# P of the row tile that TensorE turns over, kept as float32 in a range of its own, with float32 products for its columns

## The chip, the core and the metric

One NeuronCore of a Trainium2 chip runs the kernel alone. Times are device microseconds from start to end of an execution. The engines are named as the profile names them: PE (TensorE; PEld is its weight load), DVE (VectorE), ACT (ScalarE), POOL (GpSimd) and SP, whose queue issues all DMAs.

## What is computed

Attention over 2 batches and 8 heads of 768 positions of width 64, in which a query sees only the keys of its own hash bucket, and then two feed-forward layers over the 1536 tokens.

```python
q_bits = (einsum('bhsd,dk->bhsk', q, proj) > 0); k_bits = (einsum('bhsd,dk->bhsk', k, proj) > 0)
mask = q_bucket[:, :, :, None] == k_bucket[:, :, None, :]
scores = where(mask, scale * matmul(q, k.T), -1e9)
attn = exp(scores - max(scores)); attn = attn / (sum(attn) + 1e-09)
x = matmul(attn, v)                      # then [1536, 512]
h = x @ w_in;  g = maximum(0.01 * h, h);  x = g @ w_out
h = x @ w_in2; g = maximum(h, 0) + alpha * minimum(h, 0);  out = g @ w_out2
```

All inputs are float32, except that the weights come as 64-bit words which the kernel converts itself.

## The kernel before

The heads go in eight pairs (`NP`, index `i`), the two heads of a pair being `j` = 0 and 1. For each pair `load` fetches q, k and V, `split_qk` splits q and k in high and low parts, `turn` transposes them on PE (tp), and `bits` makes the bucket bits (bp). `split_v` scales V by a power of two and splits it into two float16 tiles (vb: high, low). `score` is called 12 times per pair, once per tile of 128 rows and head; three row tiles (`t` = 0, 1, 2) make a half `f` of the positions. One score is four matmuls into PSUM (sc, L685), a minimum on DVE that also moves the tile to SBUF as s (L692), and an exp in place on ACT (L695).

P must lie with the keys on the partitions for the product with V. Two of three row tiles are split into a high and a low float16 part on ACT, POOL or DVE (hl; L734, L740 and the helpers at L399 and L402) and transposed by a DMA (L746). The third, marked "T" in `HI_ON` (t = 2; in the last half of the last pair also t = 1, by `HI_LAST`), is turned over by PE: three transposes of 128 columns into a PSUM tile (pp, L711), of which there is one; then ACT writes the high float16 part out of PSUM (L715), and DVE the low one, which is the difference (L719). All three row tiles share the tile pt, [128, 24, 384] float16, whose last axis is the rows.

`pv` multiplies: for each of the six blocks of 128 keys, three float16 products (V high by P high, V low by P high, V high by P low), each for both heads, of 384 columns (L778). The heads write partitions 0 to 63 and 64 to 127 of one PSUM tile (o). The inverse row sums are laid along by three transposes (pr, L769), scaled on ACT together with the powers of two of V and P (rs, L772), and DVE multiplies o by rs into x (L787).

After that come the FFN units: `convert` makes float16 high and low weights (L927 to L971), `split` does the same to x (L978, L985), `h_group` and `y_group` do the matmuls (`three`, L1029 to L1031).

The order of the work on each engine is set by a planner: every step is put in with `plan.add(claim, ways, reads, writes)`; `Plan.order` lists the steps by a model of engine times, first forwards and then in passes from the back and the front, and takes the best end. A step with several ways (vec is DVE, act ACT, gps POOL) may go to any of these engines. A `Ring` of n tiles lets the step that takes tile n + 1 wait until the first is free: there are 6 tiles of s (`SB`), 3 of pt, 1 of V's float32 tile (rv). The FFN reuses the ring of s for g and ts.

Of the kernel before, what the change touches and what calls it, by code (L numbers as in the profile page):

```python
# [9 lines left out]
F32 = mybir.dt.float32  # L10
# [24 lines left out]
LO_LAST = "P-DP-DP-D---"  # L35
SB = 6


HOP, HOP_PE, LANDING = 0.12, 0.29, 1.6
PATIENCE, PASSES = 0.2, 8  # L40

# [131 lines left out]
class Plan:  # L173
# [49 lines left out]
    def order(self):  # L223

        self.link()
        for n, op in enumerate(self.ops):
            op.n = n
        end = self.first()
        best = end, [(op.start, op.way) for op in self.ops]
        for _ in range(PASSES):  # L230
            self.late(end)
            end = self.early()
            if end < best[0]:
                best = end, [(op.start, op.way) for op in self.ops]
        for op, (op.start, op.way) in zip(self.ops, best[1]):
            pass
        self.end = best[0]
        return sorted(self.ops, key=lambda op: (op.start, op.n))

    def first(self):  # L240

        lines = Lines()
        ready = [op for op in self.ops if not op.left]
        while ready:
            found = [(lines.soonest(op, True), op) for op in ready]
            first = {}
            for (at, *_, k), op in found:
                eng = op.ways[k][0]
                first[eng] = min(first.get(eng, at), at)
            eng = min(first, key=first.get)  # L250
            (at, done, x, k), op = min(
                (f for f in found if f[1].ways[f[0][3]][0] == eng and f[0][0] <= first[eng] + PATIENCE),
                key=lambda f: (f[1].turn, f[1].claim, f[1].n),
            )
# [37 lines left out]
def lsh_attention_ffn_kernel(  # L292
# [53 lines left out]
    nat_r = dict(zip("kq", ring("nat", 1, "kq")))  # L346
    rv_r = ring("rv", 1)
    rb_r, rs_r = ring("rb", 1, ("rb", "rs"))
# [59 lines left out]
    st_raw, st_nat, st_op, st_bt, st_v = {}, {}, {}, {}, {}  # L408
    sums, pts = {}, {}

# [106 lines left out]
    def turn(i):  # L517
# [3 lines left out]
        for nm, hi, sc in (("k", 64, -scale), ("q", 0, 1.0)):  # L521
            n = st_nat.pop((nm, i))
            for j in range(2):
                a, bb = ops[j][nm + "a"], ops[j][nm + "b"]
                for f in range(2):
# [18 lines left out]
                    for dst, src, wr in to:  # L544
                        ways = [act(0.49, lambda dst=dst, src=src, sc=sc: nc.scalar.activation(
                            out=dst(), in_=src(), func=AF.Copy, scale=sc))]
                        if i == 0:
                            ways.append(vec(0.61, lambda dst=dst, src=src, sc=sc:
                                nc.vector.tensor_scalar_mul(dst(), src(), sc)))
                        plan.add(at, ways, [ps], [wr])  # L550
                    at += 0.7
                if i:
                    plan.add(
                        at,
                        dma(1.2, lambda bb=bb: bb.t[0:64].bitcast(F32),
                            lambda a=a, hi=hi: a.t[hi:hi + 64].bitcast(F32)),
                        [a], [(bb, (0, 2))],
                    )
# [55 lines left out]
    def split_v(i):  # L614
        r_ = st_raw.pop(("v", i))
        vb = v_r.new([128, 2, 2, T, D], F16, "vb")
# [22 lines left out]
        def scales():  # L639
# [13 lines left out]
             act(0.94, lambda: nc.scalar.activation(  # L653
                 out=part(0), in_=r(), func=AF.Copy, scale=c.t[:, 0:1]))],
            [r_, c], [(vb, (0, 1))],
        )
        def p_lo():
            gmul(r(), r(), c.t[:, 0:1])
            gsub(part(1), r(), part(0))

        plan.add(
            at + 2,
            [vec(1.25, lambda: nc.vector.scalar_tensor_tensor(
                out=part(1), in0=r(), scalar=c.t[:, 0:1], in1=part(0), op0=ALU.mult,
                op1=ALU.subtract), True), gps(2.6, p_lo)],
            [c, (vb, (0, 1))], [r_, (vb, (1, 2))], lean=LEAN_V,
        )

    def score(g):
# [12 lines left out]
        def go():  # L682
# [14 lines left out]
            accum_out=sm.t[:, t, j:j + 1])), [mn], [s, (sm, (2 * t + j, 2 * t + j + 1))])  # L697
        hi_eng, lo_eng = (HI_ON[m], LO_ON[m]) if i < NP - 1 else (HI_LAST[m], LO_LAST[m])
        ts = slice(t * 128, t * 128 + 128)
        if hi_eng == "T":  # L700
            for h in range(2):
                ps = p_ps.new([128, TH, 128], F32, "pp")
                c0 = 2 * T * j + h * TH

                def hi(c0=c0):
                    return pt.t[:, c0:c0 + TH, ts]

                def over(ps=ps, h=h):
                    for c in range(TH):
# [21 lines left out]
        if lo_eng == "P":  # L731
# [3 lines left out]
                "P": gps(0.84, lambda: gmul(hi(), s.t, by))}  # L735
        plan.add(g + 1, [ways["A"]] if lo_eng == "P" else list(ways.values()), [s], [hw])
        if lo_eng == "P":
# [5 lines left out]
        if j == 1:  # L743
            plan.add(
                g + 2,
                ("SP", 3.7, 4.0, lambda: nc.sync.dma_start_transpose(  # L746
                    out=pt.t[:, :, ts], in_=hl.t.rearrange("p j s -> p (j s)"))),
                [hl], [(pt, (64 * t, 64 * t + 64))],
            )

    def pv(i, f):
# [14 lines left out]
        def along():  # L766
# [450 lines left out]
```

## Time and profile before

| what | us |
|---|---|
| median of 3 runs | 777.45 (775.96 to 778.15) |
| profiled execution | 779.42 |
| its span, first to last instruction | 777.6 |
| PE busy | 729.4 (94%) |
| DVE busy | 606.0 (78%) |
| ACT busy | 478.2 (61%) |
| POOL busy | 316.1 (41%) |

The span has two parts: attention up to about 265 us, where four engines and the DMAs work side by side, and the FFN after that. Shares over the whole span mix the two, so the rows below go by stretches. Matmuls are pipelined: the duration of one is longer than the distance from its start to the start of the next, so a run of them is read from start to start.

### The profile page before, as it was taken

The page shows a single profiled execution, that of the slowest core. Times are in us where ns is not written, and L with a number is a line of the kernel's source. Part 1 is how long each engine was busy: PE and PEld are TensorE (multiplying, and loading weights), DVE is VectorE, ACT ScalarE, POOL GpSimd, SP SyncE. Part 2 cuts the span into 40 slices and gives each one's busy share as a digit, 9 for nine tenths or more (in the row PEclk, how much of TensorE's full clock was granted, in tenths as well). Part 3 has the DMA queues.
Part 4 walks back from the last instruction along what each step waited for, and adds up shares of the span by engine and source line. Part 5 has one row for each costly group of instructions (what it writes and reads, how often), then busy time and mean ns, then how long its engine had stood idle before and what let it go on. Part 6 is the DMA issues. An engine that isn't in the chain of part 4 may idle for free.

```text
span 777.6 us, 12424 instructions
## 1 busy us (share of the span) xinstructions
PE 729.4 (94%) x4465; PEld 461.4 (59%) x4465; DVE 606.0 (78%) x1196; ACT 478.2 (61%) x923; POOL 316.1 (41%) x345
## 2 busy tenths in 40 slices
PE   7888988899978689999999999999999999999997
PEld 6676757777755346666666666565555555555553
DVE  5998979899998998787787876998687777853332
ACT  5988778788878556655434434556776664554341
POOL 3896667767543242434322233232322222222221
PEclk8999999999989899999999999999999999999999
DMA  6699879987957531222403303020140320000112
GB/s 183 147 198 200 169 150 197 195 166 148 197 101 186 152 109 45 92 82 78 140 1 110 109 1 103 25 90 0 55 136 28 109 81 28 28 1 1 42 40 82
DMA packets 131213, 77.87 MB, mean 100 GB/s; under 512 B 100864, under 2 KB 123392, under 8 KB 131152
## 3 DMA queue, kind: packets, MB, share of 16 engines
q1 hardware_dynamic: 131152, 77.08, 39.5%
q8 instruction: 35, 0.57, 0.3%
q14 instruction: 26, 0.21, 0.1%
HBM read 43.00 MB, written 3.15 MB: 59 GB/s over the span
## 4 chain that ended last, share of the span: by engine, by line
PE 77%; DVE 13%; ACT 4%; DMA 2%; issue 2%; POOL 1%; SPq 0%; ACTq 0%; DVEq 0%
PE y L1029 11%; PE y L1031 11%; PE y L1030 11%; PE h L1029 10%; PE h L1031 10%; PE h L1030 10%; PE o L778 5%; PE sc L685 4%; DVE s L692 3%; PE bp L569 2%; PE pp L711 2%; DMA pt<-hl 2%; ACT s L695 1%; PE tp L530 1%; DVE pt L719 1%
## 5 line engine op out<-in xcount | busy, mean ns | idle before, releaser
L402 POOL TENSOR_TENSOR gs<-ts,gs 128x384 f16<-128x384 f32 x128 | 122.6, 959 | 314.1 <-ACT gs L1064 249.4
L1029 PE MATMUL h<-x,wn 128*128 128x384 f16 x512 | 167.6, 327 | 5.2 <-DVE ts L1052 3.9
L1030 PE MATMUL h<-x,wn 128*128 128x384 f16 x512 | 167.5, 327 | 0.0
L1031 PE MATMUL h<-x,wn 128*128 128x384 f16 x512 | 167.4, 327 | 0.0
L1064 ACT CAST gs<-ts 128x384 f16<-128x384 f32 x128 | 65.3, 511 | 51.5 <-DVE ts L1061 27.9
L695 ACT ACTIVATE s<-s,mn 128x768 f32<-128x768 f32 x96 | 89.4, 932 | 8.7 <-DVE s L692 8.5
L692 DVE TENSOR_SCALAR_CACHE_REDUCE s<-sc 128x768 f32<-128x768 f32 x96 | 89.6, 948 | 3.8 <-PE sc L685 3.4
L1061 DVE SCALAR_TENSOR_TENSOR ts<-ts,nal 128x384 f32<-128x384 f32 x64 | 39.5, 616 | 64.8 <-ACT ts L1057 40.4
L1029 PE MATMUL y<-gs,wp 128*128 128x384 f16 x256 | 83.5, 326 | 0.0
L1030 PE MATMUL y<-gs,wp 128*128 128x384 f16 x256 | 83.5, 326 | 0.0
L1031 PE MATMUL y<-gs,wp 128*128 128x384 f16 x256 | 83.5, 326 | 0.0
L1100 DVE SCALAR_TENSOR_TENSOR x<-y,back,x 128x384 f32<-128x384 f32 (+1 forms) x84 | 56.6, 674 | 33.0 <-PE y L1031 32.5
L1050 ACT ACTIVATE ts<-h 128x384 f32<-128x384 f32 x64 | 31.0, 487 | 74.2 <-PE h L1031 59.8
L1030 PEld LDWEIGHTS <-wn 128*128 128x128 f16 x512 | 50.3, 98 | 40.6 <-issue 6.0
L1029 PE MATMUL y<-wp,gs 128*128 128x512 f16 x192 | 72.8, 379 | 0.0
L1030 PE MATMUL y<-wp,gs 128*128 128x512 f16 x192 | 72.8, 379 | 0.0
L1031 PE MATMUL y<-wp,gs 128*128 128x512 f16 x192 | 72.8, 379 | 0.0
L1029 PEld LDWEIGHTS <-wn 128*128 128x128 f16 x512 | 50.2, 98 | 35.5 <-issue 0.6
L1031 PEld LDWEIGHTS <-wn 128*128 128x128 f16 x512 | 50.3, 98 | 33.4 <-issue 0.5
L685 PE MATMUL sc<-ka,qa 128*128 128x384 f32 x192 | 58.2, 385 | 10.2 <-DVE s L692 9.8
L402 POOL TENSOR_TENSOR hl<-s,hl 128x768 f16<-128x768 f32 x31 | 54.2, 1750 | 30.9 <-ACT hl L734 30.7
L1057 ACT ACTIVATE ts<-h,al_s 128x384 f32<-128x384 f32 x64 | 37.0, 577 | 44.6 <-PE h L1031 25.0
(154 smaller groups left out, 1475.4 us busy)
## 6 DMA issues: line engine op xcount, KB each, us to landing
wr<-in_moe_w_out_dram SPq DMA_DIRECT2D x19, 512.0 KB
wr<-in_moe_w_in_dram SPq DMA_DIRECT2D x17, 512.0 KB
r<-in_moe_w_in_dram SPq DMA_DIRECT2D x15, 512.0 KB
r<-in_moe_w_out_dram SPq DMA_DIRECT2D x13, 512.0 KB
v<-in_v_dram SPq DMA_DIRECT2D x8, 384.0 KB
out_dram<-x SPq DMA_DIRECT2D x12, 256.0 KB
k<-in_k_dram SPq DMA_DIRECT2D x7, 384.0 KB
q<-in_q_dram SPq DMA_DIRECT2D x7, 384.0 KB
```

The lines of the kernel that those rows point to most:

```text
L402: nc.gpsimd.tensor_tensor(out=o, in0=a, in1=b, op=ALU.subtract)
L685: nc.tensor.matmul(sc.t[:, h, 0:HALF], lhsT=o[a].t[0:rows, row:row + 128], rhs=o[b].t[0:rows, h * HALF:h * HALF + HALF], start=(n == 0), s ...
L692: plan.add(g, vec(1.03, lambda: nc.vector.tensor_scalar(out=s.t.rearrange("p (a b) -> p a b", a=2), in0=sc.t[:, :, 0:HALF], scalar1=FILL, ...
L695: plan.add(g, act(1.12, lambda: nc.scalar.activation(out=s.t, in_=s.t, func=AF.Exp, scale=-1.0, bias=mn.t[:, 0:1], accum_out=sm.t[:, t, j: ...
L778: nc.tensor.matmul(ps.t[64 * j:64 * j + 64], lhsT=vb.t[:, piece, j, c, :], rhs=pt.t[:, 2 * T * j + o + c, :], start=(c + n == 0), stop=(c ...
L1029: nc.tensor.matmul(ps, lhsT=lh[0], rhs=rh[0], start=first, stop=False)
L1030: nc.tensor.matmul(ps, lhsT=lh[0], rhs=rh[1], start=False, stop=False)
L1031: nc.tensor.matmul(ps, lhsT=lh[1], rhs=rh[0], start=False, stop=last)
L1057: plan.add(claim, act(0.58, lambda: nc.scalar.activation(out=g.ap(F32), in_=ps.t, func=AF.Relu, scale=al_s.t[:, 0:1])), [ps, al_s], [g.use()])
L1061: plan.add(claim, vec(0.57, lambda: nc.vector.scalar_tensor_tensor(out=g.ap(F32), in0=lo.ap(F32), scalar=nal.t[:, f:f + 1], in1=g.ap(F32), ...
L1064: plan.add(claim, act(0.51, lambda: nc.scalar.copy(out=gh.ap(), in_=g.ap(F32))), [g.use()], [gh.use()])
L1100: plan.add(claim, vec(0.69 if l else 0.56, lambda: nc.vector.scalar_tensor_tensor(out=a(), in0=ps(), scalar=c(), in1=a(), op0=ALU.mult, op ...
```

## The change

A turned row tile of P is no longer split. It stays float32 in an unbroken range of pt, the bytes that its two float16 parts would fill, so `whole` sees them as [128, 12, 128] float32. The tiles that the DMA transposes are packed in front of them (`narrow`, `kept` of them, 128 columns each). After the three transposes there is one copy out of PSUM on ACT (`FP` = 0), and no step on DVE.

In `pv` the six float16 products of a block of keys go over the `kept` columns only, 256 of 384 (128 in the last half of the last pair). For each turned row tile two products follow, one per head, with V's raw float32 tile (v32) as weights and the float32 P as columns. Since neither is scaled there, the inverse row sums are scaled in two pieces, by inv for the first columns and by 1 for the rest, each on ACT or DVE (`FR` = 1).

V's float32 tile now lives until the products, so its ring has 2 tiles; the ring of s has 5 instead of 6, which also makes the slots of g 8 instead of 10. V's low part loses its way over POOL, which overwrote the raw tile. The planner now tries six values of `PATIENCE` with six passes each, where it had one value and eight passes, and it keeps the best. The options `FT`, `FH`, `FV` and `FB` are 0 and leave their lists of ways as they were.

```diff
-SB = 6
+SB = 5
+FT, FP, FR, FH, FV, FB = 0, 0, 1, 0, 0, 0
...
-PATIENCE, PASSES = 0.2, 8
+PATIENCE, PASSES = (0.05, 0.1, 0.15, 0.2, 0.25, 0.3), 7
...
-    rv_r = ring("rv", 1)
+    rv_r = ring("rv", 2)
...
+    def kept(i, f):
+
+        return sum(engines(i)[0][6 * f + m] != "T" for m in range(6)) // 2
+
+    def narrow(pt, i, f):
+
+        n = 128 * kept(i, f)
+        return pt.t.rearrange("p a b -> p (a b)")[:, 0:4 * T * n].rearrange("p (a b) -> p a b", a=4 * T)
+
+    def whole(pt, t):
+
+        flat = pt.t.rearrange("p a b -> p (a b)")[:, 4 * T * 128 * t:4 * T * 128 * (t + 1)]
+        return flat.bitcast(F32).rearrange("p (a b) -> p a b", a=2 * T)
...
-                w = (t * 64 + c0, t * 64 + c0 + TH)
-                plan.add(g + 1 + h / 2, act(0.49, lambda ps=ps, hi=hi: nc.scalar.mul(hi(), ps.t, PSCALE)),
-                         [ps], [(pt, w)])
-                plan.add(
-                    g + 1.4 + h / 2,
-                    vec(0.56, lambda ps=ps, hi=hi, c0=c0: nc.vector.scalar_tensor_tensor(
-                        out=pt.t[:, c0 + T:c0 + T + TH, ts], in0=ps.t, scalar=PSCALE, in1=hi(),
-                        op0=ALU.mult, op1=ALU.subtract)),
-                    [ps, (pt, w)], [(pt, (w[0] + T, w[1] + T))],
-                )
+                w = [(pt, (t * 64 + 2 * c0, t * 64 + 2 * (c0 + TH)))]
+                plan.add(g + 1 + h / 2, [
+                    act(0.49, lambda ps=ps, out=out: nc.scalar.copy(out=out(), in_=ps.t)),
+                    vec(0.56, lambda ps=ps, out=out: nc.vector.tensor_copy(out(), ps.t)),
+                ][:1 + FP], [ps], w)
...
-        plan.add(at, act(0.58, lambda: nc.scalar.activation(
-            out=rs.t, in_=pr.t, func=AF.Copy, scale=inv.t[:, i:i + 1])), [pr, (inv, (i, i + 1))], [rs])
+        split = 128 * kept(i, f)
+        for c0, c1 in ((0, split), (split, HALF)):
+            by = lambda c0=c0: inv.t[:, i:i + 1] if c0 == 0 else 1.0
+            dur = 0.26 + (c1 - c0) * 0.00083
+            plan.add(at, [
+                act(dur, lambda c0=c0, c1=c1, by=by: nc.scalar.activation(
+                    out=rs.t[:, c0:c1], in_=pr.t[:, c0:c1], func=AF.Copy, scale=by())),
+                vec(dur, lambda c0=c0, c1=c1, by=by: nc.vector.tensor_scalar_mul(
+                    rs.t[:, c0:c1], pr.t[:, c0:c1], by())),
+            ][:1 + FR], [pr, (inv, (i, i + 1))], [(rs, (c0, c1))])
+        v32 = st_v32[i]
...
-                            ps.t[64 * j:64 * j + 64],
+                            ps.t[64 * j:64 * j + 64, 0:split],
...
-                            rhs=pt.t[:, 2 * T * j + o + c, :],
+                            rhs=narrow(pt, i, f)[:, 2 * T * j + o + c],
...
-            plan.add(at + c / 4, pe(0.49, go), [vb, pt], [ps])
+                for t in range(split // 128, TH):
+                    for j in range(2):
+                        nc.tensor.matmul(
+                            ps.t[64 * j:64 * j + 64, t * 128:t * 128 + 128],
+                            lhsT=v32.t[:, j, c, :], rhs=whole(pt, t)[:, T * j + c],
+                            start=False, stop=(c == T - 1), skip_group_check=True,
+                        )
+
+            plan.add(at + c / 4, pe(0.55 + 0.025 * (TH - split // 128), go), [vb, pt, v32], [ps])
```

The planner's new order moves steps everywhere. On DVE, in the second pair of heads, this stands in the kernel before (s,mn<-sc is a score's minimum, pt<-pp the low half of a turned tile, hl<-s,hl that of a tile for the DMA, x<-o,rs the end of a block of products):

```order
L740 SCALAR_TENSOR_TENSOR hl<-s,hl 128x768
L663 SCALAR_TENSOR_TENSOR vb<-v,c,vb 128x768
L719 SCALAR_TENSOR_TENSOR pt<-pp,pt 128x3x128
L579 TENSOR_SCALAR bt<-bp,least,weight 128x384 x2
L692 TENSOR_SCALAR s,mn<-sc 128x768
L761 RECIPROCAL sum<-sum 128x6
L787 TENSOR_TENSOR x_1_125<-o,rs 128x384
L692 TENSOR_SCALAR s,mn<-sc 128x768
L719 SCALAR_TENSOR_TENSOR pt<-pp,pt 128x3x128
L692 TENSOR_SCALAR s,mn<-sc 128x768
```

and this about the same place in the changed one:

```order
L755 SCALAR_TENSOR_TENSOR hl<-s,hl 128x768
L776 RECIPROCAL sum<-sum 128x6
L971 SCALAR_TENSOR_TENSOR r<-r 128x512
L586 TENSOR_SCALAR bt<-bp,least,weight 128x384 x2
L712 TENSOR_SCALAR s,mn<-sc 128x768
L818 TENSOR_TENSOR x_1_125<-o,rs 128x384
L712 TENSOR_SCALAR s,mn<-sc 128x768
L794 TENSOR_SCALAR rs<-pr,inv 128x256
L712 TENSOR_SCALAR s,mn<-sc 128x768
```

The low halves pt<-pp are gone from the row, and scalings of the row sums (rs<-pr,inv) and an integer pass over a weight tile (r<-r) stand in it. Counted over the whole order, DVE has 68 pt<-pp less, 12 rs of 256 columns and 10 of 128 more, and 5 vb<-v,c, 2 x splits and a few casts more.

On PE, the end of a step of a block of products in the kernel before:

```order
L778 LDWEIGHTS vb
L778 MATMUL o<-pt,vb 64x384
L711 MATMUL pp<-ident,s 128x128 x3
L530 MATMUL tp<-ident,kn 128x128 x3
L530 MATMUL tp<-ident,qn 128x128 x3
L685 MATMUL sc<-ka,qa 128x384 x2
```

and in the changed one:

```order
L802 LDWEIGHTS vb
L802 MATMUL o<-pt,vb 64x256
L811 MATMUL o<-pt,v 64x128 x2
L705 MATMUL sc<-ka,qa 128x384 x2
L705 MATMUL sc<-kb,qb 128x384 x2
L533 MATMUL tp<-ident,kn 128x128 x3
L731 MATMUL pp<-ident,s 128x128 x3
```

The float16 products are 256 columns wide instead of 384, and two float32 ones (o<-pt,v) follow each six. Steps of a block, which mostly stood in one run of 36, now often have scores and transposes between them. In the FFN, h and y groups follow each other on PE nearly as they did.

At the end of attention, DVE ahead of the splits of the first FFN weights (wn<-r,by,wn; wr and m are the integer passes of later weights), in the kernel before:

```order
L895 TENSOR_SCALAR by<-biggest 128x1
L898 TENSOR_SCALAR by<-by 128x1
L934 TENSOR_SCALAR m<-m 128x512
L719 SCALAR_TENSOR_TENSOR pt<-pp,pt 128x3x128
L971 SCALAR_TENSOR_TENSOR wn<-r,by,wn 128x512 x3
L971 SCALAR_TENSOR_TENSOR wn<-wr,by,wn 128x512
L937 SCALAR_TENSOR_TENSOR wr<-wr,m 128x512
L940 SCALAR_TENSOR_TENSOR wr<-wr 128x512
```

and in the changed one:

```order
L926 TENSOR_SCALAR by<-biggest 128x1
L929 TENSOR_SCALAR by<-by 128x1
L968 SCALAR_TENSOR_TENSOR wr<-wr,m 128x512
L971 SCALAR_TENSOR_TENSOR wr<-wr 128x512
L1002 SCALAR_TENSOR_TENSOR wn<-r,by,wn 128x512 x3
L1002 SCALAR_TENSOR_TENSOR wn<-wr,by,wn 128x512
L960 TENSOR_SCALAR m<-m 128x512
```

The last low half is gone, and two integer passes over wr moved ahead of the splits.

## Rows read from the trace of the kernel before

**Rows 1.** Stretches A:B; busy us (and instructions) per engine, granted clock, DMA share, GB/s

```profile
20.00:240.00 220.00, 193.84 (x1371) 152.92 (x1372) 198.91 (x395) 180.78 (x366) 151.18 (x143) 0.96 0.83 169
...
300.00:400.00 100.00, 100.00 (x619) 60.50 (x618) 82.01 (x156) 53.22 (x99) 36.15 (x38) 1.00 0.26 85
400.00:700.00 300.00, 299.67 (x1726) 168.85 (x1724) 235.23 (x477) 168.43 (x313) 85.22 (x95) 1.00 0.18 59
```

**Rows 2.** Waits of PE from 20 to 240 us: total us, times, longest

```profile
PE sc L685 <- DVE s L692: 8.1, 8, 2.7
PE pp L711 <- DVE pt L719: 5.6, 9, 1.0
PE o L778 <- DMA pt<-hl: 2.3, 2, 2.1
```

**Rows 3.** Waits of DVE from 20 to 260 us

```profile
DVE x L787 <- PE o L778: 10.0, 10, 3.1
DVE s L692 <- PE sc L685: 3.4, 9, 0.8
```

**Rows 4.** Groups by line and form: xcount | busy us, mean ns; the first from 20 to 240 us

```profile
L719 DVE SCALAR_TENSOR_TENSOR pt<-pp,pt 128x384 f16<-128x384 f32 x59 | 32.4, 549 | 5.3 <-ACT pt L715 4.9
...
L734 ACT ACTIVATE hl<-s 128x768 f16<-128x768 f32 x44 | 36.5, 838 | 3.5 <-DMA pt<-hl 1.8 <-POOL s L399 1.4
L772 ACT ACTIVATE rs<-pr,inv 128x384 f32<-128x384 f32 x16 | 9.2, 578 | 2.3 <-PE pr L769 1.7 <-ACT hl L734 0.6
L985 DVE SCALAR_TENSOR_TENSOR x<-x,x_by,x 128x384 f16<-128x384 f32 x10 | 7.3, 736 | 0.0
L653 ACT ACTIVATE vb<-v,c 128x768 f16<-128x768 f32 x6 | 5.7, 945 | 0.0
L640 DVE TENSOR_REDUCE c<-vp 128x1 f32<-128x128 f32 x8 | 2.3, 287 | 0.1
L549 DVE TENSOR_SCALAR qa<-tp 128x384 fp32r<-128x384 f32 x2 | 1.1, 558 | 0.9 <-PE tp L530 0.8
L609 ACT ACTIVATE dg<-ident,mx 128x128 fp32r<-128x128 f32 x2 | 0.8, 396 | 0.2 <-DVE mx L883 0.2
L651 DVE TENSOR_SCALAR vb<-v,c 128x768 f16<-128x768 f32 x1 | 0.6, 614 | 0.0
```

**Rows 5.** Pieces of the chain that ended last: start us, us, what

```profile
19.01 0.89 DVE s L692 x2
...
97.78 7.89 DMA pt<-hl
...
120.47 0.55 PE pp L711 x3
121.02 1.39 PE bp L569 x8
122.41 1.40 PE sc L685 x8
123.81 3.05 PE o L778 x36
...
247.96 0.88 DVE s L692 x2
```

**Rows 6.** PE in order of time: start us, us

```profile
44.47 0.49 PE L711 MATMUL pp<-ident,s 128*128 128x128 f32 x3
44.80 0.97 PE L530 MATMUL tp<-ident,kn 128*128 128x128 f32 x6
45.52 0.60 PE L685 MATMUL sc<-ka,qa 128*128 128x384 f32 x2
```

**Rows 7.** The end of attention, PE and DVE in order of time

```profile
265.12 0.34 PE L1029 MATMUL h<-x,wn 128*128 128x384 f16 x1
...
263.80 0.76 DVE L971 SCALAR_TENSOR_TENSOR wn<-wr,by,wn 128x512 f16<-128x512 f32 x1
264.47 0.70 DVE L937 SCALAR_TENSOR_TENSOR wr<-wr,m 128x512 int32<-128x512 int32 x1
```

More of the change, by code (lines that the diff above doesn't have):

```diff
@@ L225, in order, with first @@
         self.link()
[L226 to L235, printed above, removed]
+        left = [op.left for op in self.ops]
+        best = None
+        for patience in PATIENCE:
+            for n, (op, op.left) in enumerate(zip(self.ops, left)):
+                op.n = n
+            end = self.first(patience)
+            for again in range(PASSES):
+                if best is None or end < best[0]:
+                    best = end, [(op.start, op.done, op.way) for op in self.ops]
+                if again < PASSES - 1:
+                    self.late(end)
+                    end = self.early()
+        for op, (op.start, op.done, op.way) in zip(self.ops, best[1]):
             pass
-        self.end = best[0]
         return sorted(self.ops, key=lambda op: (op.start, op.n))
-    def first(self):
+    def first(self, patience):
         lines = Lines()
@@ L251, in first @@
             (at, done, x, k), op = min(
-                (f for f in found if f[1].ways[f[0][3]][0] == eng and f[0][0] <= first[eng] + PATIENCE),
+                (f for f in found if f[1].ways[f[0][3]][0] == eng and f[0][0] <= first[eng] + patience),
                 key=lambda f: (f[1].turn, f[1].claim, f[1].n),
@@ L408, in lsh_attention_ffn_kernel @@
     st_raw, st_nat, st_op, st_bt, st_v = {}, {}, {}, {}, {}
-    sums, pts = {}, {}
+    sums, pts, st_v32 = {}, {}, {}
     def load(i, nm, claim, parts=1):
@@ L546, in turn @@
                             out=dst(), in_=src(), func=AF.Copy, scale=sc))]
-                        if i == 0:
+                        if i == 0 or FT:
                             ways.append(vec(0.61, lambda dst=dst, src=src, sc=sc:
@@ L554, in turn @@
                         at,
-                        dma(1.2, lambda bb=bb: bb.t[0:64].bitcast(F32),
-                            lambda a=a, hi=hi: a.t[hi:hi + 64].bitcast(F32)),
+                        [dma(1.2, lambda bb=bb: bb.t[0:64].bitcast(F32),
+                             lambda a=a, hi=hi: a.t[hi:hi + 64].bitcast(F32)),
+                         gps(0.85, lambda bb=bb, a=a, hi=hi: gmul(
+                             bb.t[0:64], a.t[hi:hi + 64].bitcast(F32), 1.0)),
+                         vec(0.5, lambda bb=bb, a=a, hi=hi: nc.vector.tensor_copy(
+                             bb.t[0:64], a.t[hi:hi + 64].bitcast(F32)), True)][:1 + FB],
                         [a], [(bb, (0, 2))],
@@ L614, in split_v @@
     def split_v(i):
-        r_ = st_raw.pop(("v", i))
+        r_ = st_v32[i] = st_raw.pop(("v", i))
         vb = v_r.new([128, 2, 2, T, D], F16, "vb")
@@ L653, in split_v @@
              act(0.94, lambda: nc.scalar.activation(
-                 out=part(0), in_=r(), func=AF.Copy, scale=c.t[:, 0:1]))],
+                 out=part(0), in_=r(), func=AF.Copy, scale=c.t[:, 0:1]))][:2 + FV],
             [r_, c], [(vb, (0, 1))],
         )
-        def p_lo():
-            gmul(r(), r(), c.t[:, 0:1])
-            gsub(part(1), r(), part(0))
         plan.add(
@@ L664, in split_v, with engines @@
                 out=part(1), in0=r(), scalar=c.t[:, 0:1], in1=part(0), op0=ALU.mult,
-                op1=ALU.subtract), True), gps(2.6, p_lo)],
-            [c, (vb, (0, 1))], [r_, (vb, (1, 2))], lean=LEAN_V,
-        )
+                op1=ALU.subtract), True)],
+            [c, r_, (vb, (0, 1))], [(vb, (1, 2))], lean=LEAN_V,
+        )
+    def engines(i):
+        return (HI_ON, LO_ON) if i < NP - 1 else (HI_LAST, LO_LAST)
+    def kept(i, f):
[6 more added lines that the diff above has]
+        return flat.bitcast(F32).rearrange("p (a b) -> p a b", a=2 * T)
     def score(g):
@@ L697, in score @@
             accum_out=sm.t[:, t, j:j + 1])), [mn], [s, (sm, (2 * t + j, 2 * t + j + 1))])
-        hi_eng, lo_eng = (HI_ON[m], LO_ON[m]) if i < NP - 1 else (HI_LAST[m], LO_LAST[m])
+        hi_eng, lo_eng = (e[m] for e in engines(i))
         ts = slice(t * 128, t * 128 + 128)
@@ L702, in score, with out @@
                 ps = p_ps.new([128, TH, 128], F32, "pp")
-                c0 = 2 * T * j + h * TH
-                def hi(c0=c0):
-                    return pt.t[:, c0:c0 + TH, ts]
+                c0 = T * j + h * TH
+                def out(c0=c0):
+                    return whole(pt, t)[:, c0:c0 + TH]
                 def over(ps=ps, h=h):
@@ L735, in score @@
                 "P": gps(0.84, lambda: gmul(hi(), s.t, by))}
-        plan.add(g + 1, [ways["A"]] if lo_eng == "P" else list(ways.values()), [s], [hw])
+        plan.add(g + 1, [ways["A"]] if lo_eng == "P" and not FH else list(ways.values()), [s], [hw])
         if lo_eng == "P":
@@ L746, in score @@
                 ("SP", 3.7, 4.0, lambda: nc.sync.dma_start_transpose(
-                    out=pt.t[:, :, ts], in_=hl.t.rearrange("p j s -> p (j s)"))),
+                    out=narrow(pt, i, f)[:, :, ts], in_=hl.t.rearrange("p j s -> p (j s)"))),
                 [hl], [(pt, (64 * t, 64 * t + 64))],
```

## Prediction

> **What bounds the kernel now.** I read the table of stretches first [rows 1]. From 300 us on PE is busy for the whole of every stretch: the two FFN layers run at TensorE's pace, and no edit here touches their matmuls. From 20 to 240 us, attention, no engine is full: DVE is the busiest with 198.9 of 220 us (0.904), PE shows 193.8, ACT 180.8, the DMA engines are busy 0.83 of the time. The waits of PE [rows 2] say who sets the pace there: the score matmuls wait 8.1 us for DVE's minimum (it empties their PSUM tile), the transposes 5.6 us for DVE's low halves of P, and DMA only 2.3 us. DVE itself waits for the scores 3.4 us and for the products 10.0 [rows 3]. So attention is bound by DVE, with PE close behind.
>
> A pair of heads takes, from the first minimum to the last over 96 scores [rows 5], (248.8 - 19.0) / 8 = 28.7 us. DVE's share of it is 0.904 x 28.7 = 25.9 us, DMA's 0.83 x 28.7 = 23.8, ACT's 180.8 / 220 x 28.7 = 23.6. PE's busy figure holds the drain of every isolated matmul, so I count its need from start to start in unbroken runs: 8 score or bit matmuls take 1.40 us and 36 products with V 3.05 [rows 5], 3 float32 transposes 0.33 and 6 of them 0.72 [rows 6], that is 0.115 each. A pair has 48 score matmuls (8.4 us), 16 for the bits (2.8), 72 products (6.1) and 54 transposes (6.2): 23.5 us.
>
> **What the change does to each engine.** DVE loses the 68 low halves at L719, 0.549 us each [rows 4]: -37.3 us. It gains 12 scalings of 256 columns of the row sums and 10 of 128, which the planner now may give to it. For 128 columns out of PSUM I take 0.29 us (the maximum over 128 columns at L640), for 384 it is 0.56 (L549), for 256 halfway, 0.42 [rows 4]: 12 x 0.42 + 10 x 0.29 = 7.9 us. Five more high halves of V at 0.614 (L651) are 3.1, and two more x splits at 0.74 (L985) with a few casts some 2.5. Net -23.8 us. Of the low halves 59 lie between 20 and 240 us (32.4 us), and some 11.5 us of the gains: -20.9 in 220 / 28.7 = 7.7 pairs, 2.7 each, and 25.9 becomes 23.2. The other nine belong to the tail below.
>
> ACT keeps its 68 copies out of PSUM at the old duration. It loses 16 scalings of the row sums at 0.578 and 6 high halves of V at 0.945 (-14.9 us), and gains 10 narrower scalings (0.3 to 0.5 each, estimated between L640 and L772, 4 in all), 4 high halves of P at 0.838 (3.4) and 6 diagonals at 0.396 (2.4) [rows 4]. Net -5, 0.6 per pair: 23.0. POOL gives work away (332 instructions for 350) and was never near its limit.
>
> PE: each of the 6 steps over keys in a product block issued six matmuls of 384 columns, 3.05 / 6 = 0.51 us. Now the six are 256 columns wide and two float32 products of 128 columns follow. If the six scale with their columns they take 0.34; weight loads could keep them higher, which the float32 price below has room for. A real float32 product is in no row of before. Lower end: the float32 operands of the scores, 1.40 / 8 for 384 columns, go through in one pass, so two products of 128 columns that ran side by side like the halves of the f16 pairs would take 0.06. Upper end: two transposes of three, each started alone, 0.55 / 3 apiece [rows 5], 0.37. The nearest row is the run of float32 transposes, two at 0.12 = 0.24 [rows 6], and I take that: +0.07 per step, 102 pairs of products in all, 7 us, 0.85 per pair of heads. PE becomes 24.3, between 22.2 and 25.9 by the ends.
>
> The score matmuls show float32 operands at one pass [rows 5]. The Trainium skill (FP8 and Floating Point Precision, TensorE Precision Notes) says that true float32 takes four passes through the array, against one for reduced precision; by it 4 x 128 columns would go where 3 x 128 went, 0.23 for the pair if the two column halves still overlap, +0.06 a step or 6 us in all. The trace shows no true float32 product that could agree or not.
>
> The other edits. The ring of s goes from 6 tiles to 5: a tile is now free for the minimum five scores later, 5 x 2.4 = 12 us, where it was 14. POOL, which reads s last in one tile of three, is named by none of DVE's waits in attention [rows 3], so I cost it at nothing; if that spare time is gone, the minimum waits and PE's next score behind it. In the FFN 10 slots of g become 8: PE's order still takes an h group and a y group in turn, and the last y that reads a slot stands ahead of the h that refills it two units later, so nothing. A second buffer for V's float32 tile lets its load run while the products still read the old one; nothing. At the start k and q are now issued ahead of the projection, under 1 us, which I do not count. At PE's end of attention the eight turned pieces no longer wait for DVE's low half, but the first FFN matmul at 265.1 comes right after DVE's weight split of 263.8 [rows 7]. DVE has nine low halves less there (5 us), and by the order two integer passes of a weight tile (0.70 each [rows 7]) more ahead of the splits. I take 1.5 us of the 3.6, since the x splits and weight passes stay in the same row on DVE.
>
> **The sum.** After the change the four needs per pair are PE 24.3, DMA 23.8 (the same transfers), DVE 23.2, ACT 23.0. DVE filled 0.904 of the pair when the next was 0.07 lower; with four within 0.05 of each other more of them will meet, and I take 0.885: 24.3 / 0.885 = 27.4 us, 1.3 less, times 8 is 10.5. With the tail 12 us. The profiled execution took 779.4 us (span 777.6), so 767.4; the median of the runs shown lies 1.97 below it, and in its terms the forecast is 765.5.
>
> **The rivals.** *More comes back.* Most of PE's idle time hangs on DVE [rows 2]; if PE alone sets the pace and reaches 0.95, a pair takes 25.6 and 8 x 3.1 + 1.5 = 26 us go, 751.5 in the median's terms; half of that surplus gives 758. Against it: DMA's 23.8 then needs 0.93. *DMA takes over.* The chain holds stretches of a transposed P on its way, the longest 7.9 us [rows 5], and no transfer is removed; DMA's 0.83 is then what a queue in order can reach, the pair stays 28.7 and only the tail is won: 776. For it: those stretches. Against it: PE waits only 2.3 us for it in all [rows 2]. *Slower: the float32 products run one after the other.* Six f16 products of 384 columns take 0.51 us, so two side by side take 0.17, and 0.057 for 128 columns. If a float32 product goes through four times, as four half products, and the two column halves do not overlap, the pair costs 8 x 0.057 = 0.45: PE needs 23.5 + 12 x 0.28 = 26.9, at 0.885 30.4 per pair, 8 x 1.7 - 1.5 = 12 more, 789.5. It decides against the change from the point where PE's need at 0.885 passes 28.7, 25.4 us, which is a pair of products at 0.33. (The four passes of the Trainium skill's page above lead here when the halves do not overlap, and to the forecast when they do.) That the change does not do what it says I rule out: the order shows 68 low halves gone and 204 float32 products added.
>
> **How the numbers follow.** A measurement of this kernel tells 0.3% (2.3 us) from no change. Forecast, 7 to 17 us less: 0.53. More comes back: 0.17. DMA takes over in part, 2.3 to 7 less: 0.08; in full, within 0.3%: 0.10. Slower: 0.12. So faster 0.78, same 0.10, slower 0.12. The range reaches from 752, nearly all of the second case, to 779, which takes in the DMA case and the float32 price up to 0.35; the slow rival's own time stays outside.
>
> **What would show it.** In the profile of the changed kernel: no DVE group pt<-pp; DVE below 0.85 of the attention stretch; two float32 products of one step within 0.2 to 0.28 us; six f16 ones in about 0.34; the last minimum near 238 us and the first FFN matmul near 253; FFN stretches still full of PE. The forecast is wrong if a pair of float32 products takes over 0.33 us, if waits of the products for transposed P grow by several us, or if minima begin to wait for the smaller ring of s.

## The result, and the profile after

The changed kernel takes 771.88 us (median of 5 runs, 770.01 to 772.71) where the kernel before took 776.14 beside it (5 runs): a ratio of 0.9915, 95% interval 0.9887 to 0.9943. It is faster, as forecast, and inside the range, but by 4.3 us where 12 were forecast. The medians' own ratio would be 0.9945; by the ratio on record the gain is 6.6 us. The two profiled executions stand 7.2 us apart, 772.2 against 779.4 (spans 770.4 and 777.6). So the gain is 4 to 7 us, and a difference of 2 or 3 us between the changed kernel and a run below is not told from nothing. What follows splits the two spans.

| | before | after | difference |
|---|---|---|---|
| start to the first minimum | 18.9 | 18.2 | -0.7 |
| first minimum to end of the last | 229.9 | 226.3 | -3.6 |
| end of the last minimum to first h matmul (the tail) | 16.3 | 20.2 | +3.9 |
| first h matmul to the end (the FFN) | 512.5 | 505.7 | -6.8 |

What attention wins between its minima the tail loses again; the gain that is left stands in the FFN, whose arithmetic the change does not touch.

The table of stretches after answers to [rows 1]; its columns are the same (PE, PEld, DVE, ACT, POOL, granted clock, DMA share, GB/s):

```profile
20.00:240.00 220.00, 200.41 (x1718) 169.59 (x1717) 184.46 (x373) 178.91 (x371) 152.02 (x137) 0.98 0.86 169
240.00:265.00 25.00, 16.98 (x186) 13.72 (x185) 23.49 (x54) 18.41 (x37) 6.40 (x7) 0.80 0.81 212
265.00:300.00 35.00, 34.13 (x212) 20.52 (x210) 31.94 (x61) 20.02 (x38) 11.44 (x14) 1.00 0.18 61
```

and the two stretches of before that the rows ahead of the prediction left out:

```profile
240.00:265.00 25.00, 17.62 (x125) 11.29 (x123) 23.39 (x56) 20.31 (x41) 9.96 (x13) 0.86 0.65 164
265.00:300.00 35.00, 29.59 (x173) 16.96 (x170) 31.66 (x59) 18.57 (x35) 11.39 (x13) 0.95 0.32 109
```

DVE fell from 198.9 to 184.5 us of 220, PE rose to 200.4, the DMA share to 0.86. No engine took DVE's place: the fullest is PE with 0.91 (0.88 before), and its busy figure holds the drain of isolated matmuls. From 265 to 300 us PE is busy for 34.1 of 35 us, where before it was idle for 5.4. From 300 us on PE is full as before.

The waits from 20 to 240 us, of PE (answering to [rows 2]) and of DVE ([rows 3] has those of before, up to 260 us): total us, times, longest.

```profile
PE sc L705 <- DVE s L712: 4.2, 10, 0.8
PE pp L731 <- ACT s L715: 2.9, 5, 0.8
PE tp L533 <- DVE rs L794: 2.6, 3, 1.4
PE o L802 <- DMA pt<-hl: 2.2, 3, 1.1
PE pr L784 <- POOL rb L777: 2.0, 3, 0.9
...
DVE s L712 <- PE sc L705: 13.7, 21, 2.3
DVE bt L586 <- PE bp L576: 5.0, 5, 1.4
DVE s L712 <- POOL hl L405: 3.5, 5, 1.4
```

DVE now waits for PE's scores (13.7, before 3.2 in the same stretch), PE's wait for the low halves is gone, and five minima wait for POOL, which reads the tile of s that they need: the smaller ring, which I had costed at nothing. The chain of waits up to 260 us gives 16.0% to transposed P on its way (5.3% before), in stretches like these (start, us, what):

```profile
150.77 7.96 DMA pt<-hl
...
163.47 7.97 DMA pt<-hl
```

PE in order of time, two steps of products (start, us; a float32 product shows as two records, so x4 is one pair), and two steps of the last half, where two row tiles are turned:

```profile
60.72 0.52 PE L802 MATMUL o<-pt,vb 128*64 128x256 f16 x6
61.07 0.39 PE L811 MATMUL o<-pt,v 128*64 128x128 f32 x4
61.28 0.49 PE L802 MATMUL o<-pt,vb 128*64 128x256 f16 x6
61.61 0.39 PE L811 MATMUL o<-pt,v 128*64 128x128 f32 x4
...
263.36 0.33 PE L802 MATMUL o<-pt,vb 128*64 128x128 f16 x6
263.52 0.61 PE L811 MATMUL o<-pt,v 128*64 128x128 f32 x8
263.96 0.33 PE L802 MATMUL o<-pt,vb 128*64 128x128 f16 x6
```

The six float16 products take 0.33 us (61.28 to 61.61), the pair of float32 ones 0.21 (61.07 to 61.28), two pairs 0.44.

The groups that the change added (by form, 20 to 240 us), and the copy that stayed on ACT:

```profile
L736 ACT COPY pt<-pp 128x384 f32<-128x384 f32 x60 | 28.4, 473 | 18.8 <-PE pp L731 18.6
...
L794 DVE TENSOR_SCALAR rs<-pr,inv 128x256 f32<-128x256 f32 x12 | 5.7, 478 | 0.1
L658 DVE TENSOR_SCALAR vb<-v,c 128x768 f16<-128x768 f32 x6 | 5.1, 857 | 0.1
L794 DVE TENSOR_SCALAR rs<-pr 128x128 f32<-128x128 f32 x10 | 2.8, 283 | 1.0 <-ACT rs L792 1.0
```

The end of attention, PE and then ACT in order of time (before: [rows 7]):

```profile
258.22 0.90 PE L731 MATMUL pp<-ident,s 128*128 128x128 f32 x3 [3.81 <-ACT pt L736]
259.05 0.53 PE L802 MATMUL o<-pt,vb 128*64 128x128 f16 x6
...
260.23 0.53 PE L802 MATMUL o<-pt,vb 128*64 128x128 f16 x6
...
264.67 0.34 PE L1060 MATMUL h<-x,wn 128*128 128x384 f16 x1
...
254.54 2.07 ACT L995 ACTIVATE wn<-r,by 128x512 f16<-128x512 f32 x3 [0.57 <-DVE by L929]
256.52 0.74 ACT L995 ACTIVATE wn<-wr,by 128x512 f16<-128x512 f32 x1
257.16 0.65 ACT L958 ACTIVATE m<-wr 128x512 f32<-128x512 f32 x1
257.71 0.45 ACT L736 COPY pt<-pp 128x384 f32<-128x384 f32 x1
```

PE waits 3.8 us for a copy of pp that stands behind four weight splits and a cast in ACT's queue. After that wait the first steps of products go at 1.18 us a step (259.05 to 260.23), at a granted clock of 0.50 (258.2 to 262.6 us), TensorE's lower level of 1.2 GHz; the last ones take 0.60.

### The profile page after: what moved, and what is told of

Its sections match the earlier page's. It is cut to its first block, busy times and chain, and to the rows that moved or that the text cites. A ratio compares the mean times of both kernels' runs of the same rounds, so it can differ in the third digit from the quotient of the medians.

```text
span 770.4 us, 13177 instructions
## 1 busy us (share of the span) xinstructions
PE 735.1 (95%) x4873; PEld 480.9 (62%) x4873; DVE 590.0 (77%) x1162; ACT 471.4 (61%) x919; POOL 306.0 (40%) x327
## 4 chain that ended last, share of the span: by engine, by line
PE 76%; DVE 8%; DMA 6%; issue 3%; ACT 3%; POOL 3%; SPq 0%; DVEq 0%; POOLq 0%; ACTq 0%
PE h L1060 11%; PE h L1062 11%; PE h L1061 11%; PE y L1060 11%; PE y L1061 11%; PE y L1062 11%; DMA pt<-hl 5%; PE sc L705 3%; PE o L802 2%; DVE s L712 2%; PE bp L576 2%; PE o L811 2%; PE tp L533 2%; POOL hl L405 2%; DVE hl L755 1%
## 5 line engine op out<-in xcount | busy, mean ns | idle before, releaser
L712 DVE TENSOR_SCALAR_CACHE_REDUCE s<-sc 128x768 f32<-128x768 f32 x96 | 90.0, 951 | 18.1 <-PE sc L705 13.7
L405 POOL TENSOR_TENSOR hl<-s,hl 128x768 f16<-128x768 f32 x31 | 56.2, 1815 | 17.6 <-ACT hl L749 17.5
```

The lines of the kernel that those rows point to most:

```text
L405: nc.gpsimd.tensor_tensor(out=o, in0=a, in1=b, op=ALU.subtract)
L712: plan.add(g, vec(1.03, lambda: nc.vector.tensor_scalar(out=s.t.rearrange("p (a b) -> p a b", a=2), in0=sc.t[:, :, 0:HALF], scalar1=FILL, ...
```

## The experiments

The questions are what freeing DVE brings by itself, and what takes the rest. Each run below was timed beside the kernel before on its own chip, so ratios are compared; the changed kernel's is 0.9915.

**The planner apart from the arithmetic.** The change holds a wider search too. Before with that search alone (and the loop over its values, which is not shown):

```diff
-PATIENCE, PASSES = 0.2, 8
+PATIENCE, PASSES = (0.05, 0.1, 0.15, 0.2, 0.25, 0.3), 7
...
```

> The kernel before, with only the planner's wider search (six values of PATIENCE, six passes each). Theory A (the 4 to 7 us came from DVE losing the 68 low halves): no change beyond 0.3%, 774 to 779 us. Rival B (the new order of the wider search is what gained): 769 to 773 us.

786.32 us, ratio 1.0096 (1.0060 to 1.0132). And the change with one value of `PATIENCE` and as many passes as before:

```diff
-PATIENCE, PASSES = (0.05, 0.1, 0.15, 0.2, 0.25, 0.3), 7
+PATIENCE, PASSES = (0.2,), 9
```

> The changed kernel with the old search (PATIENCE 0.2 alone, the same eight passes). Theory A: it keeps the gain, 769 to 775 us. Rival B: it is back at 775 us or over.

786.91 us, ratio 1.0095 (1.0065 to 1.0125). By the profiled spans: with the old search the new arithmetic goes from 777.6 to 783.4, with the wide one from 784.0 to 770.4. Each half of the change alone, in the order that it got, makes the kernel slower. The stretch from 20 to 240 us of the second kernel:

```profile
20.00:240.00 220.00, 196.03 (x1653) 168.02 (x1653) 172.47 (x355) 172.29 (x359) 148.20 (x141) 0.96 0.85 167
```

and DVE's waits in it:

```profile
DVE s L712 <- POOL hl L405: 7.1, 5, 2.0
DVE hl L755 <- POOL hl L402: 4.8, 2, 2.4
```

No engine there is fuller than in the changed kernel, and the last minimum ends 4.7 us later (249.2 against 244.5), with more waits for POOL. The larger part of the 13 us is behind attention: the FFN takes 515.9 us against 505.7, and PE waits there once for 7.1 us for ACT's dg. So the planner's order is worth as much as the arithmetic, in either sign, and a comparison is clean only with the order held. Of each kernel below the text says whether it is.

**DVE's work given back.** Once as a planned step, so that the planner makes a new order:

```diff
+                plan.add(g + 1.4 + h / 2, vec(0.56, lambda ps=ps, out=out: nc.vector.tensor_copy(out(), ps.t)),
+                         [ps], w)
```

> The changed kernel in which DVE copies each turned tile out of PSUM once more after ACT, the same values to the same place, planned at 0.56 us: DVE's 68 instructions are back, the float32 products stay. Theory A: DVE is the bound again, with 13 us more than before, and the time goes over 776 us, to 776 to 784. Rival C (DVE had room left and something else bounds the changed kernel, so that its relief is worth little): under 774 us.

779.23 us, ratio 1.0012 (0.9986 to 1.0037): the gain is gone, with DVE at 198.3 of 220 us. The order is another one too, so this run alone does not say which of the two took the gain. And once inside ACT's step, so that the order is the changed kernel's word for word:

```diff
-act(0.49, lambda ps=ps, out=out: nc.scalar.copy(out=out(), in_=ps.t)),
+act(0.49, lambda ps=ps, out=out: (nc.scalar.copy(out=out(), in_=ps.t),
+    nc.vector.tensor_copy(out(), ps.t))),
```

> The order of the changed kernel word for word, but behind each of ACT's 68 copies of a turned tile DVE copies the same values to the same place once more (0.55 us each, 37 us in all), which the planner does not know of. So nothing but DVE's load and the later freeing of pp differs. Theory A (within one order the relief of DVE is worth what the sum said): 12 to 25 us over the changed kernel, 784 to 797. Rival C (DVE had room, the gain is an accident of the order): less than 6 us over it, under 778.

796.66 us, ratio 1.0238 (1.0216 to 1.0261). Waits of PE there, 20 to 240 us:

```profile
PE pp L731 <- DVE pt L737: 14.7, 13, 2.7
PE sc L705 <- DVE s L712: 4.3, 9, 0.9
```

The wait that the change removed is back, larger, and the run costs 25 us: 15 of them stand between the minima, 9 in the tail. Over the whole run PE waits 24.5 us for these copies, while the scores' wait for the minima is as before (4.3, in the changed kernel 4.2). That a DVE step on the one tile of pp holds PE up is shown, within one order. Whether it does so because DVE is loaded or because the tile comes free later, this run does not separate.

**DVE's work taken from before.** The order of before, the low halves and a third of the columns of their product left out in all pairs but the last:

```diff
-vec(0.56, lambda ps=ps, hi=hi, c0=c0: nc.vector.scalar_tensor_tensor(
+vec(0.56, (lambda: None) if i < NP - 1 else lambda ps=ps, hi=hi, c0=c0: nc.vector.scalar_tensor_tensor(
...
+n_ = lambda n: 256 if n == 2 and i < NP - 1 else HALF
...
```

> The order of the kernel before word for word; DVE's low halves of turned tiles are left out in all pairs but the last (56 of 68, 31 us of DVE), and the third product covers the 256 other columns only (PE 5 us less), so P of the turned tiles is float16 alone. Theory A (DVE bounds the kernel before): 10 to 20 us under it, 758 to 768. Rival C: less than 5 us under it.

772.86 us, ratio 0.9927 (0.9899 to 0.9955). The stretch from 20 to 240 us, and waits of DVE and of PE in it:

```profile
20.00:240.00 220.00, 190.79 (x1388) 156.11 (x1387) 178.46 (x348) 184.19 (x376) 158.17 (x145) 0.96 0.87 172
```

```profile
DVE s L692 <- PE sc L685: 17.4, 25, 2.0
DVE x L789 <- PE o L780: 8.0, 8, 3.2
...
PE pp L711 <- ACT s L695: 7.4, 11, 2.0
PE sc L685 <- DVE s L692: 7.1, 8, 1.7
```

Some 31 us of DVE and 5 of PE are gone, no float32 product has come, and no order has moved; the kernel gains 5.7 us by its ratio. DVE now idles for scores (17.4, before 3.2 in this stretch), and PE waits for the minima almost as long as before (7.1, before 8.1), and longer for ACT's exp (7.4, before 4.6). So DVE freed in a fixed order brings 6 us at most, not 10 to 20. The time is near the changed kernel's, but not in the same places: between the minima this kernel wins 4.6 us and the changed one 3.6, while in the FFN it wins 0.9 and the changed one 6.8.

**PE's work doubled and removed**, in the changed kernel's order. Float32 products twice:

```diff
-                    for j in range(2):
+                    for j in (0, 1, 0, 1):
```

> The changed kernel's order word for word; each float32 product is issued twice, so the columns of turned tiles come out doubled. PE gets 102 x 0.22 = 22 us more. Theory P (PE is the next bound, as the sum had it): 15 to 22 us over the changed kernel, 787 to 794. Rival Q (the DMA queue took over): 3 to 10 us over it, 775 to 782.

788.31 us, ratio 1.0125 (1.0103 to 1.0146). Float32 products for the first block of keys only:

```diff
-                for t in range(split // 128, TH):
+                for t in range(split // 128, TH) if c == 0 else ():
...
```

> The changed kernel's order word for word; the float32 products are left out for all but the first of the six blocks of keys, 17 of 102 pairs stay, so PE has 85 x 0.22 = 19 us less. Theory P: 10 to 19 us under the changed kernel, 753 to 762. Rival Q: 1 to 6 us under it, 766 to 771.

767.52 us, ratio 0.9866 (0.9832 to 0.9901). Twice the products, some 22 us of PE, cost 16; five sixths less, some 18 us, return 4, with an interval that touches the changed kernel's. PE binds when loaded further, but in this order float32 products at no cost would have brought only some 4 us more.

**How the float32 products go through.** In every other block of keys each float32 product is issued twice in a row, two on one column half and then two on the other; the blocks between have none:

```diff
-                    for j in range(2):
+                    for j in (0, 0, 1, 1) if c % 2 == 0 else ():
...
```

> The cost of a float32 product by itself: the order of the changed kernel, but the products of two blocks of keys stand together in the even blocks and come as head 0, 0, 1, 1 instead of 0, 1, with the odd blocks left out, so the columns of turned tiles are wrong and the number of products is the same. If a product's passes run side by side with those of the other head's column half: four products take 0.6 to 0.9 us instead of 0.44. If every pass goes alone: 0.42 to 0.46 us as now.

One execution, 768.85 us. PE in order of time:

```profile
59.25 0.66 PE L811 MATMUL o<-pt,v 128*64 128x128 f32 x8
59.69 0.88 PE L802 MATMUL o<-pt,vb 128*64 128x256 f16 x12
```

Four products take 0.44 us (59.25 to 59.69) with neighbours on the same half, as two pairs do on alternate halves: a product takes 0.11, one after the other, and nothing overlaps.

**The DMA queue.** The stretches of the chain made it the next suspect. Three runs in the changed kernel's order tried it. The 28 copies of rows of qa and ka done by POOL instead of a DMA:

```diff
-[dma(1.2, lambda bb=bb: bb.t[0:64].bitcast(F32),
-     lambda a=a, hi=hi: a.t[hi:hi + 64].bitcast(F32)),
+[("SP", 0.45, 1.2, lambda bb=bb, a=a, hi=hi: gmul(
+     bb.t[0:64], a.t[hi:hi + 64].bitcast(F32), 1.0)),
```

> The changed kernel's order word for word; the 28 copies of 192 KB from the a to the b operands (ka to kb, qa to qb) are done by POOL at the place where SP issued them, so the DMA queue carries 28 transfers less and POOL has some 28 x 0.85 = 24 us more, which the planner does not know of. Rival Q (the DMA queue bounds): 3 to 8 us under the changed kernel, 764 to 769. Theory P: within 3 us of it or slower, 769 to 780.

784.49 us, ratio 1.0069 (1.0040 to 1.0098), the DMA share 0.68. POOL became late (166.1 of 220 us busy; PE waits 8.8 us for its rb, 2.0 in the changed kernel), so the run says nothing on the DMAs. The copies left out from the second pair on, the second score matmul reading only the 12 rows of the bits, which begin at partition 64:

```diff
-[dma(1.2, lambda bb=bb: bb.t[0:64].bitcast(F32),
-     lambda a=a, hi=hi: a.t[hi:hi + 64].bitcast(F32)),
+[("SP", 0.45, 1.2, lambda: None),
...
-for n, (a, b, rows) in enumerate((("qa", "ka", 128), ("qb", "kb", 64 + NR))):
+for n, (a, b, rows) in enumerate((("qa", "ka", slice(0, 128)), ("qb", "kb", slice(64 if i else 0, 64 + NR)))):
...
```

> The changed kernel's order word for word; the 28 copies of 192 KB from the a to the b operands are left out for all pairs but the first, and the second score matmul of those pairs reads only the 12 rows of the bits (same columns, so the same PE time), so the products of the low parts of q and k are missing. No engine gets work in their place, unlike the run before in which POOL did them. Rival Q (the DMA queue holds the changed kernel): 4 to 9 us under the changed kernel, 762 to 768. Otherwise (DMA is hidden): within 2.5 us of it, 769 to 774.

786.50 us, ratio 1.0104 (1.0056 to 1.0151), the DMA share 0.66, and PE at 211.0 of 220 us. A score there up to the next one's start, and one of the changed kernel:

```profile
103.44 0.59 PE L704 MATMUL sc<-ka,qa 128*128 128x384 f32 x2
103.96 0.61 PE L704 MATMUL sc<-kb,qb 12*128 12x384 f32 x2
104.50 0.62 PE L704 MATMUL sc<-ka,qa 128*128 128x384 f32 x2
```

```profile
58.60 0.62 PE L705 MATMUL sc<-ka,qa 128*128 128x384 f32 x2
59.06 0.52 PE L705 MATMUL sc<-kb,qb 76*128 76x384 f32 x2
59.48 0.62 PE L705 MATMUL sc<-ka,qa 128*128 128x384 f32 x2
```

A score takes 1.06 us from start to start where it took 0.88: the 12 rows from partition 64 made PE slower, and the run is no test of the DMAs either. The last run keeps all shapes on PE and cuts the copies' bytes to a third:

```diff
-[dma(1.2, lambda bb=bb: bb.t[0:64].bitcast(F32),
-     lambda a=a, hi=hi: a.t[hi:hi + 64].bitcast(F32)),
+[dma(1.2, lambda bb=bb, w=w: bb.t[0:64, 0:w].bitcast(F32),
+     lambda a=a, hi=hi, w=w: a.t[hi:hi + 64, 0:w].bitcast(F32)),
...
+                    r_, h_ = (0, 0) if i and n else (row, h)
```

> The changed kernel, its order word for word, with the 28 transfers that copy 64 rows of qa and ka into qb and kb cut to a third of their bytes from the second pair on (128 of 768 columns for q, 384 for k). The second matmuls of a score then always read the first 128 columns of qb and the first 384 of kb, so what they add is right for the first tiles alone; their shapes stay 76 rows by 128 and by 384 columns, unlike in the run without copies, where 12 rows made PE slower. PE, DVE, ACT and POOL do what they do in the changed kernel. Theory B (after the change the DMA engines and their queue are the next limit: 0.86 of 20 to 240 us busy, 16% of the chain a transposed P on its way): the busy share of the DMAs falls to 0.72 to 0.78, the stretches pt<-hl of the chain shrink, attention ends 5 to 15 us earlier, so 757 to 768 where the changed kernel takes 771. Theory C (four in-order queues tied to each other by a fixed order; no one resource is the limit): the DMA share falls as much, but the time stays within 3 us of the changed kernel's, and other waits (DVE for scores, PE for the minimum) take the place.

770.17 us, ratio 0.9895 (0.9869 to 0.9921). The stretch from 20 to 240 us, and DVE's waits in it:

```profile
20.00:240.00 220.00, 199.69 (x1726) 169.51 (x1726) 185.34 (x376) 180.70 (x374) 153.89 (x139) 0.99 0.78 154
```

```profile
DVE s L714 <- PE sc L707: 12.4, 22, 2.0
...
DVE s L714 <- POOL hl L405: 4.0, 5, 1.4
```

The share fell from 0.86 to 0.78, and the time by 1.5 us against the changed kernel's ratio, which its interval does not tell from nothing. Theory B's 5 to 15 us are not there: in this order the DMAs are not the next limit by their load. How long one transposed tile is on its way was not tried by itself.

**The tail.** The copies of pp of the last pair may go to DVE as well:

```diff
-                ][:1 + FP], [ps], w)
+                ][:2 if i == NP - 1 else 1], [ps], w)
```

> The changed kernel in which the copies of turned tiles of the last pair alone may go to DVE too, so that they need not stand behind ACT's four weight splits. Theory D (the end of attention gave 4 us back, 3.8 of them in PE's wait for one copy that stands behind the weight splits on ACT): 767 to 770 us, first FFN matmul 2 to 4 us earlier after the last minimum. Rival E (DVE's weight passes set that end and only the waiting engine changes): 771 to 774 us.

770.13 us, ratio 0.9892 (0.9842 to 0.9943). From the last minimum to the first h matmul it takes 17.3 us (20.2 in the changed kernel), but the planner made another order for the whole of attention, and the FFN part is 5.3 us longer, so this is no proof of the tail's cause. It is the fastest complete kernel by its median, not separable from the changed one.

## Why the prediction was right, and where it was off

The sign is right and the time lies in the range, but the path to it is another, and in part luck. A gain of 2.3 to 7 us, which the medians and the ratio both give, had a chance of 0.08 and a cause, the DMAs, that the runs do not confirm. Without the FFN's 6.8 us, which the sum had at nothing, the change would have come out within half a microsecond of the kernel before.

- **DVE held PE up: right for the low halves, not for the minima.** Giving DVE its work back in the same order cost 25 us, and the wait pp<-DVE pt (5.6 us) is gone from the changed kernel. The larger of the two waits that the prediction read, 8.1 us of the scores for the minima, did not come from the low halves: with 31 us of them gone in the order of before it is still 7.1.
- **PE's price: right.** The pair of float32 products takes 0.21 us (taken: 0.24), the six float16 ones 0.33 (0.34), a step 0.55 against 0.51. Summed over PE's rows in order of time, each run to the start of the next matmul and without the last half of the last pair, whose first steps went at the lower clock, the products with V go from 50.4 to 56.1 us, +5.7 where +7 was taken for all, though they now lie in 42 unbroken runs where there were 29, and a step alone takes 0.66. The slower rival is out by its own test: 0.21 is below its 0.33. Its mechanism is half true: the halves do not overlap, but a product goes through as two records, not four.
- **DVE's balance: size off.** The scalings take 478 ns for 256 columns (taken 420) and the high halves of V 857 (taken 614). DVE ended 14.5 us lower in the stretch, not 20.9; by 240 us it has also done 93 minima where it had done 91. The run without low halves freed more (31 us) and gained little more than the change did, so this is not what was missing.
- **The packing: the step that failed.** "24.3 / 0.885 = 27.4 us, 1.3 less" for a pair of heads. Measured: 226.3 / 8 = 28.3, 0.45 less; by the measured price PE's need is 24.2 and its share of the pair 0.86, not 0.885. I took it that engines would fill a pair about as well when four of them need nearly the same. In the runs the sensitivity is one-sided. With an order held, DVE loaded by 38 us costs 25 (changed order, all of it steps on the one tile of pp), and relieved by 31 returns 6 (order of before); PE loaded by 22 costs 16, and relieved by 18 returns 4; the DMAs relieved by 0.08 of their share return 1.5, not told from nothing. Each engine takes its work in a fixed order and waits for others in turn, so one that is relieved waits for the next (DVE for scores, 13.7 us) and the time stays. This is Theory C of the run with small copies, which the numbers bear out there; that no single wait remains to be lifted is argued from these runs, not shown for every resource. An order made for one load need not suit another, so a planner that knew of a relief might win more by it; that is not separated here.
- **The order: not in the sum at all.** I treated the planner's new order as carrying the same work. By the two runs of the search it moves the span by +6.4 in the old arithmetic and by -13.0 in the new one, about as much as the whole effect or more. Between the minima the orders made for the changed arithmetic take 226.3, 232.7 and 222.5 us (the changed kernel, the old search, the last pair's copies free to go to DVE), those for the old one 229.9 and 238.5.
- **Ring of s at nothing: not borne out.** Five minima wait 3.5 us for POOL, which the prediction had named as a sign of being wrong. What that costs at the end was not measured alone.
- **The tail, -1.5: wrong sign.** It is 3.9 us longer. The turned pieces no longer wait for DVE, but the one PSUM tile of pp now waits for ACT alone, and the weight splits stand in ACT's queue ahead of its copy (3.8 us). That these splits are the cause was not tried with the order held.
- **The FFN at nothing: wrong, and it paid for the tail.** PE's first 35 us there had 4.5 us more work in them. Of the 6.8 us, these waits of before are 5.2:

```profile
PE h L1029 <- DVE ts L1052: 3.9, 2, 2.4
...
PE h L1029 <- DVE x L787: 1.3, 1, 1.3
```

The steps waited for, ts and x, stand on DVE between passes over weights, and DVE is busy almost without a gap there (265 to 282 us). The first split of the second layer's weights, before and after:

```profile
279.32 2.08 DVE L971 SCALAR_TENSOR_TENSOR wp<-wr,by,wp 128x512 f16<-128x512 f32 x3 [0.17 <-ACT wp L964]
...
272.37 2.07 DVE L1002 SCALAR_TENSOR_TENSOR wp<-wr,by,wp 128x512 f16<-128x512 f32 x3
```

It starts 14.2 us after the first h matmul in the kernel before and 7.7 in the changed one, so more of the weights' passes lie ahead of the FFN. The rest of the 6.8 fits the granted clock, 0.95 before and 1.00 after from 265 to 300 us. This gain goes with the order and not with DVE's load: with the changed order the FFN takes 505.7 to 507.6 us in all eight kernels, the one with DVE's work given back among them (506.4), and in the other orders 510.4 to 515.9, the changed arithmetic with the old search among them.

"DMA takes over" is what the attention part looks like (the chain, 16.0%), and cutting the copies' bytes did not confirm it. The FFN is still full of PE, as forecast; the last minimum ended at 244.5, not 238, and the first h matmul came at 264.7, not 253.

## What to carry to other kernels

When several in-order engines are within a tenth of each other, price a relief by what the next wait allows, not by the engine's own time: here 31 us of DVE's work in attention were worth at most 6. If a planner sets the order, a change of arithmetic and a change of order have to be timed apart, each with the other held. A wait taken out of one queue should be looked for in the queue that inherits the step, here ACT's copy behind the weight splits. And a gain is to be split by stretches before it is credited to a cause: here most of it stood where nothing had been forecast.

## What was new about the hardware

- A float32 product of 64 weight columns and 128 streamed columns shows as two matmul records and takes 0.11 us. At the start of the FFN float16 products of 384 columns take 0.163 each (the changed kernel's first six: 264.67 to 265.65), so 128 columns take 0.054 and a float32 product takes the time of two passes. The Trainium skill (FP8 and Floating Point Precision, TensorE Precision Notes) says that true float32 takes four passes; these rows show two. A footnote of the Trainium skill (Perfetto Trace Analysis, Engine Utilization) halves the output rate for what it calls FP32_LOW_HIGH; the rows fit it, if these products are of that kind.
- Float16 products on the two column halves overlap (six of 256 columns in 0.33, 0.055 each, half of what 256 columns one by one would take); float32 ones do not.
- A score whose second matmuls use 12 rows from partition 64 on, instead of 76 from 0, takes 1.06 us instead of 0.88, at a granted clock of 1.00 from 100 to 120 us. The Trainium skill (TensorEngine Tiling, Array Packing, Key Properties) says that a change of the tiling mode drains TensorE. That this is what happens here is one reading; no run here shows it or separates it from others.
- In that run the granted clock stood at 0.50, the lower level of 1.2 GHz, from 58 to 66 us though PE was busy for all of it with scores, transposes and products; it was 1.00 from 50 to 55, and between the two PE stood idle once, for 0.57 us.
